# Scores of units 8 to 15 in two column halves, with q times its exponents made on POOL

## The chip, the cores and the metric

The kernel runs on one core of one Trainium2 chip. A core has TensorE (PE, matmuls; its weight loads are listed as PEld), VectorE (DVE), ScalarE (ACT), GpSimd (POOL) and SyncE (SP, which here issues DMAs alone). Each engine works through its own list of instructions in order; semaphores tie the lists together. The metric is the device time of one execution in microseconds (us). All times in the traces count from the first instruction of the profiled execution.

## The reference

A gated linear attention (mLSTM) over batch 4, 8 heads, 768 positions and head size 40, and behind it two dense two-layer networks, 320 to 2048 to 320 features, on all 3072 rows:

```python
for t in range(S):
    m_new = np.maximum(f_gate[:, :, t] + m, i_gate[:, :, t])
    f_stab = np.exp(f_gate[:, :, t] + m - m_new)
    i_stab = np.exp(i_gate[:, :, t] - m_new)
    C = f_stab[:, :, None, None] * C + i_stab[:, :, None, None] * np.einsum('bhd,bhe->bhde', vt, kt)
    n = f_stab[:, :, None] * n + i_stab[:, :, None] * kt
    h_tilde = np.einsum('bhde,bhe->bhd', C, qt)
    nq = np.einsum('bhd,bhd->bh', n, qt)[:, :, None]
    y[:, :, t] = o * h_tilde / np.maximum(np.abs(nq), 1.0)
...
h = x @ w_in;  g = h * np.clip(h + 3.0, 0.0, 6.0) / 6.0;  x = g @ w_out      # first network
h = x @ w_in;  r = np.maximum(h, 0.0);  g = r * r;        x = g @ w_out      # second network
```

## The kernel before

**Attention in units.** The 768 positions are cut into 12 chunks of 64. A unit is one chunk of one batch element, all 8 heads: 48 units, numbered so that each batch element's chunks come in order. For unit u the steps are, by their names in the code: at_qk (SP loads q and k, transposed, into the tile qkt, three buffers), at_kn and at_va (loads of k and v), w_pe and w_e up to unit 15 (PE sums gates into PSUM, ACT takes the exponent into the tile W, four buffers) or at_gload, w_add, w_mask and w_e from unit 16 on (SP, POOL, POOL, ACT), at_S (PE: the scores), at_P and x_q (fill the tile Xm, two buffers), x_k (fills its right part with k times the last exponents), at_Y (PE: Xm against the tile Z of v and carried state), at_C (copies the new state), at_n1 to at_n3 (divide, and multiply with the output gate). The first 64 rows of Xm hold the masked, weighted scores, the next 40 rows hold q times its exponents.

**Three ways to the same Xm.** Up to unit 15 (U1), at_S makes, for each head, a score product into rows 0 to 63 of the PSUM tile Sp (L448) and a product of q with an identity into rows 64 to 103 (L450), and at_P multiplies all 104 rows with W in one DVE instruction (L472). Units 16 to 21 have only the score products (L463), the even heads in rows 0 to 63 of Sp and the odd heads in rows 64 to 127, so that Sp is half as wide; at_P has two halves (L479), and x_q multiplies q and W straight out of SBUF (L412), on POOL unless FIRST says otherwise. From unit 22 (US) on the scores are made from split operands (L456).

**The two networks.** A slot s is one group of 128 hidden features for a group of rows. mm_A makes its hidden values in PSUM (ring ps_a, two tiles), act1 (ACT), act1b (DVE), act2 (ACT or DVE) and act2b (DVE) form the activation as a high and a low part, mm_B multiplies these with the second weights two slots later. act2b gives the PSUM tile of mm_A back for slots up to 23. Weights come as 64 bit numbers: w_load (SP), w_exp (ACT), w_b1 and w_b2 (DVE), w_hi (ACT or DVE), w_lo (POOL or DVE); they are all loaded while the first attention units run. The other gates' steps (gate_b:1 is L310 and L311 on DVE) and at_rg (POOL, L348) run in the same stretch.

**The order.** No scheduler chooses it. The string FIRST lists steps for the first part of the program by hand, and what is not in it follows by the rule in moe(). Each engine executes its instructions in the order in which this list names them; @v, @g and @a send a step to DVE, POOL or ACT. A tile of a ring (qkt, W, Xm, Sp) is given to a new unit when the last instruction that uses the old one is over, and the instruction that writes it first waits for that. Waits between engines are put in from the data alone.

Around the change FIRST reads, in part: "at_qk:12 act2:9@v", "at_rg:12 ... gate_b:1 ... act2:11 x_k:9@v at_kn:12 at_S:10 act1:12 w_b2:0,12 o_load:5 at_Y:9 act2b:11 x_k:10 w_hi:0,12", and later "at_S:12 ... at_qk:15 ... at_va:19 ... w_load:0,15 ... x_k:12@v w_exp:0,15 x_k:13@v at_gload:16 ... act1:18 at_Y:12 w_b1:0,15 ... act1b:18".

Of the kernel before, what the change touches and what calls it, by code (L numbers as in the profile page):

```python
# [38 lines left out]
at_Y:1 at_rg:4 w_load:0,3 at_C:0@v at_n1:0 w_load:0,10 at_n2:0@a w_load:0,9 w_pe:4 at_rg:5@v  # L39
at_kn:4 at_n1:1 at_n3:0@g at_S:2 at_n2:1 at_C:1@v x_k:2 at_va:6 w_hi:0,0 at_n3:1@g w_exp:0,1 w_pe:5  # L40
at_P:2,0 w_e:4 at_rg:6 at_S:3 w_load:0,4 at_qk:5 w_lo:0,0@v w_exp:0,7 w_b1:0,1 at_Y:2 w_e:5
w_b2:0,1 w_exp:0,2 at_qk:6 at_P:3,0 x_k:3 w_pe:6 w_hi:0,1 at_n1:2 at_rg:7 at_n2:2@a at_S:4
w_load:0,8 w_b1:0,2 w_b2:0,2 at_C:2 w_pe:7 w_exp:0,3 at_rg:8@v at_kn:5 at_P:4,0 at_n3:2@g w_hi:0,2
at_Y:3 w_e:7 w_lo:0,2 w_e:6 t_pe:0,0,0 at_n1:3 at_kn:6 w_exp:0,9 at_C:3@v w_load:0,6 t_hi:0,0,0
at_n2:3@a at_va:7 at_n3:3 t_lo:0,0,0 x_k:4 t_pe:0,0,1 w_lo:0,1 w_exp:0,10 at_Y:4 t_hi:0,0,1@v
at_va:8 t_lo:0,0,1 w_exp:0,4 at_va:9 w_b1:0,3 at_qk:7 mm_A:0 at_C:4 w_b1:0,4 at_n1:4 w_b2:0,4
mm_A:1 act1:0 at_kn:7 at_n2:4 w_hi:0,4 at_va:10 act1b:0 at_S:5 at_n3:4@g act2:0@v at_qk:8 act1:1
act2b:0 w_exp:0,8 w_lo:0,4 act1b:1 mm_A:2 at_P:5,0 act2:1 mm_B:0,1 act2b:1 act1:2 w_load:0,11
at_S:6 w_exp:0,6 w_b2:0,3 at_qk:9 mm_A:3 x_k:5@v w_hi:0,3 act1b:2 x_k:6 at_kn:8 at_Y:5 at_P:6,0
act2:2 w_load:0,5 w_lo:0,3 act1:3 mm_B:0,0 at_va:11 act2b:2 at_C:5 at_S:7 act1b:3 at_va:12 at_n1:5  # L50
act2:3 at_n2:5 x_k:7 at_qk:10 mm_A:4 at_P:7,0 at_kn:9 at_Y:6 w_exp:0,11 w_b1:0,6 load_gates:1
w_b2:0,6 w_pe:8 act1:4 mm_B:1,0 at_C:6 mm_B:2,0 act2b:3 at_rg:9 w_e:8 mm_B:1,1 act1b:4 w_hi:0,6
mm_B:2,1 at_n1:6 w_pe:9 at_rg:10 at_n2:6 act2:4 mm_B:3,1 w_exp:0,5 act2b:4 mm_B:3,0 at_n3:6 w_e:9
mm_A:5 w_b1:0,5 w_lo:0,6@v at_Y:7 act1:5 o_load:3 w_b2:0,5 at_S:8 x_k:8@a at_qk:11 at_n1:7 mm_A:6
at_P:8,0 o_load:2 at_C:7 act1b:5 w_pe:10 at_rg:11 w_hi:0,5 w_load:0,13 w_b1:0,8 o_load:1 at_n3:5
# [9 lines left out]
o_load:5 at_Y:9 act2b:11 x_k:10 w_hi:0,12 at_kn:13 at_P:10,0 mm_A:13 at_C:9 w_lo:0,12 act1b:12
at_va:17 mm_B:11,3 at_n1:9 act2:12 mm_B:11,2 at_n2:9 at_qk:13 act1:13 at_S:11 act1b:13 at_n3:9@g
act2b:12 act2:13 at_Y:10 act2b:13 at_va:18 w_b2:0,9 mm_A:14 at_C:10 gate_bT:1 w_hi:0,9 at_qk:14
mm_A:15 act1:14 x_k:11@v o_load:4 mm_B:12,2 act1b:14 w_lo:0,9 act1:15 at_kn:14 mm_B:12,3 at_P:11,0
act2:14 mm_B:13,3 mm_B:13,2 act2b:14 w_pe:12 w_b1:0,10 mm_A:16 act1b:15 at_rg:13 w_e:12 at_n1:10
act2:15 at_n2:10@a act2b:15 w_b1:0,14 at_S:12 w_b2:0,14 act1:16 mm_A:17 at_qk:15 w_b2:0,10  # L70
w_hi:0,14 act1b:16 w_lo:0,14 mm_B:14,2 at_P:12,0 act1:17 mm_B:15,2 act2:16@v mm_B:14,3 w_pe:13
act1b:17 at_rg:14 mm_B:15,3 w_e:13 act2b:16 at_Y:11 act2:17 w_hi:0,10@v w_pe:14 at_va:19 at_C:11@v
at_rg:15 mm_B:16,3 w_e:14 mm_B:16,1 at_n1:11 mm_B:16,2 at_n2:11@a w_lo:0,10 act2b:17 w_load:0,15
at_S:13 mm_B:17,3 at_P:13,0 at_qk:16 mm_B:16,0 mm_B:17,0 w_b1:0,11 w_pe:15 w_b2:0,11 mm_A:18 w_e:15
at_n3:11 w_hi:0,11 x_k:12@v w_exp:0,15 x_k:13@v at_gload:16 mm_B:17,2 at_n3:10 at_kn:15 act1:18
at_Y:12 w_b1:0,15 at_va:20 mm_A:19 act1b:18 w_lo:0,11 at_C:12 at_n1:12 at_kn:16 at_n2:12@a
at_gload:17 act2:18@v w_add:16 at_S:14 act2b:18 w_b2:0,15 mm_B:18,3 act1:19 at_qk:17 at_Y:13
w_b1:0,13 w_hi:0,15 mm_A:20 w_b2:0,13 at_va:21 at_C:13 x_k:14@a at_n1:13 w_add:17 at_n2:13 act1b:19
mm_B:17,1 w_mask:16 mm_B:18,1 at_P:14,0 act2:19 mm_B:18,0 at_kn:17 w_mask:17 mm_B:18,2 at_gload:18
w_e:16 act2b:19 at_S:15 act1:20 at_n3:12 at_n3:13 w_hi:0,13 mm_B:19,3 at_qk:18 mm_B:19,0 at_P:15,0  # L80
x_k:15@a w_lo:0,13 mm_B:19,2 act1b:20 at_S:16 at_Y:14 w_lo:0,15@v act2:20 mm_A:21 at_kn:18 at_va:22
at_n1:14 w_add:18 w_e:17 act2b:20 at_gload:19 at_C:14 at_n2:14 w_mask:18 mm_A:22 act1:21 x_q:16
# [13 lines left out]
act1b:27 act1:28 at_S:20 at_n3:19@g at_qk:23 act1b:28 mm_B:24,0 mm_B:25,0 x_k:20 at_P:20,0  # L96
mm_B:25,3 at_P:20,1 mm_B:26,0 qk_split:22 at_S:21 mm_B:26,3 mm_A:29 x_q:21@v x_k:21@a mm_B:25,1
mm_B:24,2 at_P:21,0 mm_B:25,2 act2:27@v mm_B:26,2 mm_B:26,1 act2b:27 mm_A:30 at_P:21,1 act1:29
at_kn:22 act2:28@v at_va:26 act2b:28 at_gload:23 mm_B:27,2 act1b:29 mm_B:27,3 qk_split:23 at_qk:24
mm_B:28,2 mm_A:31 act2:29 act1:30 at_S:22 act1b:30 w_add:23 at_Y:20 mm_A:32 act2b:29 at_C:20  # L100
at_n1:20 w_mask:23 act1:31 at_n2:20@a x_q:22 at_P:22,0 mm_B:29,2 act1b:31 mm_B:27,0 at_S:23
at_n3:20@g mm_B:28,0 w_e:23 at_kn:23 mm_B:29,0 x_k:22@a at_kn:24 mm_B:27,1 at_gload:24 mm_B:28,3
act2:30@v at_Y:21 at_gload:25 act2b:30 at_gload:26 mm_B:29,3 qk_split:24 mm_B:28,1 at_qk:25
mm_B:30,2 act1:32 mm_B:30,3 mm_B:29,1 act2:31 mm_B:30,0 mm_B:30,1 mm_A:33 act1b:32 w_add:24
at_n1:21 at_n2:21 w_mask:24 act2:32@v mm_A:34 w_add:25 w_e:24 at_C:21@v act2b:31 at_Y:22 act2b:32
act1:33 mm_B:31,3 at_C:22@v x_q:24 act1:34 mm_B:32,3 act1b:33 at_va:27 mm_B:31,1 mm_B:32,1 at_kn:25
act1b:34 act2:33 w_mask:25 mm_A:35 at_n1:22 w_add:26 qk_split:25 w_e:25 mm_A:36 at_n2:22 x_q:23
x_k:23@a mm_B:31,0 mm_B:32,0 at_P:23,0 at_qk:26 mm_B:31,2 t_pe:0,2,0 act2b:33 act2:34 at_Y:23
x_k:24@v t_hi:0,2,0 mm_B:33,1 act2b:34 act1:35 mm_B:33,3 mm_B:33,0 t_lo:0,2,0 at_n3:22@g at_C:23
mm_B:34,3 act1:36 act1b:35 mm_B:34,0 w_mask:26 mm_B:34,1 act1b:36 t_pe:0,2,2 mm_B:32,2 w_e:26  # L110
at_n3:21 mm_B:33,2 at_n1:23 t_hi:0,2,2 mm_B:34,2 at_n2:23 act2:35 mm_A:37 t_lo:0,2,2 at_n3:23@g
act2:36 act2b:35 t_pe:0,2,3 mm_A:38 at_qk:27 act2b:36 t_hi:0,2,3 act1:37 t_lo:0,2,3 act1b:37
t_pe:0,2,1 act1:38 mm_B:35,2 mm_A:39 t_hi:0,2,1 act1b:38 act2:37 t_lo:0,2,1 act2b:37 mm_A:40
act1:39 act1b:39 at_S:24 mm_B:35,3 at_P:24,0 qk_split:26 mm_B:35,0 at_gload:27 mm_B:35,1 at_kn:26
at_Y:24 act2:38 at_kn:27 mm_B:36,1 at_S:25 mm_B:36,2 at_n1:24 x_q:26 mm_B:37,2 at_C:24@v mm_B:37,1
at_n2:24 mm_B:36,3 act2b:38 mm_B:37,3 mm_B:36,0 at_n3:24 mm_B:37,0 act2:39@v x_q:25 x_k:25@a
x_k:26@a at_P:25,0 act2b:39
# [749 lines left out]
```

## Time and profile before

| | us |
|---|---|
| median of 3 timed runs | 842.63 (841.74 to 842.73) |
| span of the profiled execution | 839.9 |
| PE busy in it | 812.8 (97%) |
| DVE busy | 548.6 (65%) |
| ACT busy | 428.2 (51%) |
| POOL busy | 222.6 (27%) |

The span runs from the first to the last instruction of the program. A share of busy time is an average over stages: the attention units lie in the first 400 us, and the weights of the first network are prepared in the first 125 us. To read the profile for one stage, take the windows of that stage, and then the list of each engine.

### The profile page before, as it was taken

How to read it: one execution, taken by the hardware profiler on the slowest of the kernel's cores; microseconds unless marked ns; L12 is line 12 of the kernel's file. 1: busy time of each engine (PE TensorE's matmuls, PEld its weight loads, DVE VectorE, ACT ScalarE, POOL GpSimd, SP SyncE). 2: the span in 40 equal slices, each digit the busy share in tenths (PEclk: the TensorE clock that was granted, in tenths of full speed). 3: DMA queues.
4: the chain of work that ended last, by engine and by line, in shares of the span. 5: the costliest groups of instructions: out<-in, count | busy, mean ns of one | idle time of the engine just before them, and what ended most of it. 6: DMA issues, size and time to landing. Idle time of an engine off the chain costs nothing.

```text
span 839.9 us, 19200 instructions
## 1 busy us (share of the span) xinstructions
PE 812.8 (97%) x7968; PEld 719.5 (86%) x7968; DVE 548.6 (65%) x919; ACT 428.2 (51%) x815; POOL 222.6 (27%) x201
## 2 busy tenths in 40 slices
...
GB/s 240 280 150 210 108 115 80 132 87 26 123 95 117 84 112 100 87 119 7 2 81 181 197 94 1 1 33 1 32 0 1 32 1 1 32 1 1 32 1 31
DMA packets 28674, 63.59 MB, mean 76 GB/s; under 512 B 4748, under 2 KB 17100, under 8 KB 28588
## 3 DMA queue, kind: packets, MB, share of 16 engines
...
q14 instruction: 24, 0.20, 0.1%
...
## 4 chain that ended last, share of the span: by engine, by line
PE 92%; ACT 2%; DVE 2%; issue 2%; POOL 1%; DMA 0%; ACTq 0%; POOLq 0%; DVEq 0%
PE hps L639 41%; PE acc L680 39%; PE Yp L490 4%; PE tp L615 2%; PE Sp L456 2%; PE Sp L448 1%; PE Wp L372 1%; PE Sp L450 1%; PE Wp L370 1%; PE Sp L463 0%; ACT qs L432 0%; ACT X L687 0%; ACT yt L519 0%; DMA qkt<-in_qk 0%; POOL Xm L412 0%
## 5 line engine op out<-in xcount | busy, mean ns | idle before, releaser
L639 PE MATMUL hps<-xs,wi 128*128 128x512 f32 (+1 forms) x1600 | 389.4, 386 | 1.5 <-DVE xs L624 0.7
L680 PE MATMUL acc<-wo,gh 128*128 128x320 f32 x1536 | 348.2, 313 | 0.0
L639 PEld LDWEIGHTS hps<-xs,wi 128*128 128x128 f32 x1600 | 287.3, 190 | 51.1 <-DVE xs L624 1.1
L680 PEld LDWEIGHTS acc<-wo,gh 128*128 128x128 f32 x1536 | 259.1, 188 | 9.8
L680 PE MATMUL acc<-wo,gl 128*128 128x320 f32 x768 | 237.5, 309 | 0.5 <-DVE gl L670 0.5
L670 DVE TENSOR_TENSOR gl<-g,gh 128x512 fp32r<-128x512 f32 x176 | 131.1, 746 | 65.9 <-ACT gh L665 64.7
L660 DVE TENSOR_TENSOR g<-g 128x512 f32<-128x512 f32 x96 | 66.4, 691 | 127.8 <-ACT g L650 127.2
L680 PEld LDWEIGHTS acc<-wo,gl 128*128 128x128 f32 x768 | 144.4, 188 | 0.7 <-DVE gl L670 0.7
L665 ACT CAST gh<-g 128x512 fp32r<-128x512 f32 x169 | 104.6, 619 | 66.4 <-DVE g L660 53.3
L648 ACT ACTIVATE g<-hps,three 128x512 f32<-128x512 f32 (+1 forms) x104 | 68.0, 654 | 137.3 <-PE hps L639 122.0
L650 ACT ACTIVATE g<-hps 128x512 f32<-128x512 f32 x96 | 57.4, 598 | 151.6 <-PE hps L639 151.6
L657 DVE SCALAR_TENSOR_TENSOR g<-g,hps 128x512 f32<-128x512 f32 x80 | 54.7, 685 | 50.2 <-ACT g L648 50.0
L412 POOL TENSOR_TENSOR Xm<-qkt,W 40x512 f32<-40x512 f32 x31 | 40.9, 1321 | 109.2 <-ACT W L402 83.5
L600 POOL TENSOR_TENSOR wi<-wt,wi 128x768 fp32r<-128x768 f32 x14 | 26.6, 1897 | 106.9 <-ACT wi L595 101.7
L379 POOL TENSOR_TENSOR W<-W,bT 104x512 f32<-104x512 f32 x32 | 43.2, 1348 | 17.3 <-DMA W<-Gd 13.1
L490 PEld LDWEIGHTS Yp<-Z,Xm 104*32 104x32 f32 (+1 forms) x3072 | 35.0, 110 | 14.0 <-issue 11.5
L434 DVE SCALAR_TENSOR_TENSOR qs<-qs,less,qkt 120x512 fp32r<-120x512 f32 x52 | 38.0, 772 | 8.5 <-ACT qs L432 8.3
L490 PE MATMUL Yp<-Z,Xm 104*32 104x41 f32 (+1 forms) x3072 | 40.9, 209 | 1.0 <-issue 0.9
L615 PE MATMUL tp<-ident,X 128*128 128x128 f32 x144 | 24.4, 279 | 8.9 <-DVE xs L626 6.0
L600 POOL TENSOR_TENSOR wo<-wt,wo 128x640 fp32r<-128x640 f32 x15 | 24.4, 1630 | 31.5 <-ACT wo L595 31.4
L615 PEld LDWEIGHTS tp<-ident,X 128*128 128x128 f32 x144 | 18.7, 143 | 14.7 <-ACT rwi L574 6.4
L532 DVE TENSOR_TENSOR X<-X,yt 64x320 f32<-64x320 f32 x34 | 28.7, 845 | 2.5 <-ACT yt L519 1.6
...
## 6 DMA issues: line engine op xcount, KB each, us to landing
...
```

What stands on the lines that cost most here:

```text
L379: on("w_add", "g", u).tensor_tensor(out=W, in0=W, in1=bT[:, c - NC1, b * H:(b + 1) * H].unsqueeze(2).to_broadcast([KX, H, L]), op=ALU.add)
L490: nc.tensor.matmul(out=Yp[o:e, h, :], lhsT=Xm[:, h, o:e], rhs=Z[b][c % 2][:, h, :], start=True, stop=True)
L600: on("w_lo", "g", ph, i).tensor_tensor(out=w[:, 1], in0=f, in1=w[:, 0].bitcast(F32), op=ALU.subtract)
L615: nc.tensor.transpose(out=tp[:, k, :], in_=x[:, c0:c0 + P], identity=ident)
L639: nc.tensor.matmul(out=h, lhsT=w[:, hl, kk, o:o + P], rhs=t[:, xk, i0 * P:i1 * P], start=(i == 0), stop=(i == len(TERMS) - 1))
L648: nc.scalar.activation(out=g, in_=T["h", s], func=ACTF.Relu, bias=three)
L650: nc.scalar.activation(out=g, in_=T["h", s], func=ACTF.Relu)
L657: nc.vector.scalar_tensor_tensor(out=g, in0=r, scalar=6.0, in1=T["h", s], op0=ALU.min, op1=ALU.mult)
L660: nc.vector.tensor_tensor(out=g, in0=r, in1=r, op=ALU.mult)
L665: copy("act2", s)(out=gh, in_=g)
L670: nc.vector.tensor_tensor(out=gl, in0=g, in1=gh.bitcast(F32), op=ALU.subtract)
L680: nc.tensor.matmul(out=acc[i], lhsT=g[:, n], rhs=w[:, hl, m % MG, :], start=(m == 0 and q == 0), stop=(m == NM - 1 and q == 2))
```

## The change

Units 8 to 15 take the second way instead of the first: at_S without the identity products and with a half as wide Sp, at_P in two halves, and x_q as an instruction of its own on POOL. In the code the limit in at_S, at_P and x_q is the new U2 = 8 in place of U1 = 16; w_e and the other uses of U1 stay. In FIRST, x_q:u is put right in front of x_k:u, and at_P:u,1 right behind at_P:u,0, for u from 8 to 15; nothing else in the list is moved (the rest of that part of the diff is lines broken at other places).

```diff
+at_Y:1 at_rg:4 w_load:0,3 at_C:0@v at_n1:0 w_load:0,10 at_n2:0@a w_load:0,9 w_pe:4 at_rg:5@v at_kn:4
...
+w_lo:0,6@v at_Y:7 act1:5 o_load:3 w_b2:0,5 at_S:8 x_q:8 x_k:8@a at_qk:11 at_n1:7 mm_A:6 at_P:8,0
+at_P:8,1 o_load:2 at_C:7 act1b:5 w_pe:10 at_rg:11 w_hi:0,5 w_load:0,13 w_b1:0,8 o_load:1 at_n3:5
...
+w_e:11 mm_A:12 gate_b:1 mm_B:10,2 mm_B:10,3 act2:11 x_q:9 x_k:9@v at_kn:12 at_S:10 act1:12 w_b2:0,12
+o_load:5 at_Y:9 act2b:11 x_q:10 x_k:10 w_hi:0,12 at_kn:13 at_P:10,0 at_P:10,1 mm_A:13 at_C:9
...
+w_hi:0,9 at_qk:14 mm_A:15 act1:14 x_q:11 x_k:11@v o_load:4 mm_B:12,2 act1b:14 w_lo:0,9 act1:15
...
+mm_B:16,2 at_n2:11@a w_lo:0,10 act2b:17 w_load:0,15 at_S:13 mm_B:17,3 at_P:13,0 at_P:13,1 at_qk:16
+mm_B:16,0 mm_B:17,0 w_b1:0,11 w_pe:15 w_b2:0,11 mm_A:18 w_e:15 at_n3:11 w_hi:0,11 x_q:12 x_k:12@v
+w_exp:0,15 x_q:13 x_k:13@v at_gload:16 mm_B:17,2 at_n3:10 at_kn:15 act1:18 at_Y:12 w_b1:0,15
...
+w_add:16 at_S:14 act2b:18 w_b2:0,15 mm_B:18,3 act1:19 at_qk:17 at_Y:13 w_b1:0,13 w_hi:0,15 mm_A:20
+w_b2:0,13 at_va:21 at_C:13 x_q:14 x_k:14@a at_n1:13 w_add:17 at_n2:13 act1b:19 mm_B:17,1 w_mask:16
...
+at_P:15,1 x_q:15 x_k:15@a w_lo:0,13 mm_B:19,2 act1b:20 at_S:16 at_Y:14 w_lo:0,15@v act2:20 mm_A:21
...
@@ -174,6 +175,7 @@
     UL = 4
 
     US = 22
+    U2 = 8
     KS = 3 * D
...
     def x_q(u):
-        if u < U1:
+        if u < U2:
             return
...
         pool, tag = (ps_a, "a") if u in (1, 2) else (ps_s, "s")
-        if u < U1:
+        if u < U2:
 
             Sp = pool.tile([P, H, L], F32, tag=tag, name="Sp")
...
         W, Xm, Sp = T["W", u], x_tile(u), T["S", u]
-        if u < U1:
+        if u < U2:
             if o == 0:
```

## Rows read from the trace of the kernel before

**Rows 1.** Page, part 4: the chain that ended last, shares by engine.

```profile
PE 92%; ACT 2%; DVE 2%; issue 2%; POOL 1%; DMA 0%; ACTq 0%; POOLq 0%; DVEq 0%
```

**Rows 2.** Windows: stretch, length, busy PE, PEld, DVE, ACT, POOL; clock, DMA, GB/s.

```profile
77.00:92.00 15.00, 15.00 (x296) 13.65 (x295) 14.05 (x29) 10.64 (x19) 7.52 (x5) 1.00 0.34 90
...
104.00:115.00 11.00, 11.00 (x160) 8.82 (x161) 10.09 (x19) 5.85 (x18) 4.99 (x4) 1.00 0.40 127
...
72.80:76.00 3.20, 3.20 (x14) 3.20 (x15) 3.14 (x6) 3.15 (x10) 1.35 (x3) 0.52 0.92 231
```

**Rows 3.** Timeline of PE: start, length, engine, line, operation, tiles, shape, count.

```profile
85.42 0.27 PE L448 MATMUL Sp<-qkt 40*64 40x64 f32 x1
...
86.50 0.80 PE L490 MATMUL Yp<-Z,Xm 104*32 104x41 f32 x64
87.23 1.22 PE L639 MATMUL hps<-xs,wi 128*128 128x256 f32 x8
...
115.41 0.56 PE L680 MATMUL acc<-wo,gh 128*128 128x320 f32 x2
115.81 0.31 PE L680 MATMUL acc<-wo,gl 128*128 128x320 f32 x1
```

**Rows 4.** Chain of waits, in order of time: start, length, what; at_S of a later unit.

```profile
143.98 0.61 PE Sp L463 x16
```

**Rows 5.** Timeline of PE near 72 us; in brackets the idle time and its releaser.

```profile
70.44 0.55 PE L615 MATMUL tp<-ident,X 128*128 128x128 f32 x3 [2.88 <-POOL X L532]
```

**Rows 6.** Lines L472, L479, L412 by source: ns min/median/max, first and last start, shapes.

```profile
L472 DVE TENSOR_TENSOR Xm<-Sp,W x16: 673/690/693, 13.6 to 121.8; 104x512 f32<-104x512 f32 x16
...
L479 DVE TENSOR_TENSOR Xm<-Sp,W x12: 407/422/426, 126.3 to 163.6; 64x256 f32<-64x256 f32 x12
...
L412 POOL TENSOR_TENSOR Xm<-qkt,W x31: 1287/1294/1735, 126.0 to 391.9; 40x512 f32<-40x512 f32 x31
```

**Rows 7.** Timelines of POOL and DVE near 105 us.

```profile
104.60 1.84 POOL L600 TENSOR_TENSOR wi<-wt,wi 128x768 fp32r<-128x768 f32 x1
...
104.77 1.70 DVE L506 TENSOR_SCALAR rd<-rd 64x8 int32<-64x8 int32 x1
```

**Rows 8.** Timeline of DVE, 81 to 91 us.

```profile
81.56 1.26 DVE L580 TENSOR_SCALAR wt<-rwo 128x640 int32<-128x640 int32 x1
...
83.39 0.67 DVE L310 TENSOR_TENSOR X<-X,X 32x512 f32<-32x512 f32 x1
84.10 0.68 DVE L311 TENSOR_TENSOR X<-X,X 32x512 f32<-32x512 f32 x1
84.71 0.47 DVE L423 TENSOR_TENSOR Xm<-kI,W 104x320 f32<-104x320 f32 x1
...
85.98 0.41 DVE L670 TENSOR_TENSOR gl<-hps,gh 128x256 fp32r<-128x256 f32 x1
...
90.50 0.83 DVE L586 SCALAR_TENSOR_TENSOR wt<-rwo,wt 128x640 int32<-128x640 int32 x1
```

**Rows 9.** Timeline of POOL, 80 to 91 us.

```profile
80.36 2.11 POOL L348 TENSOR_TENSOR pre<-pre,Gp 64x512 fp32r<-64x512 f32 x1
82.54 0.87 POOL L423 TENSOR_TENSOR Xm<-kI,W 104x320 f32<-104x320 f32 x1
...
89.46 0.85 POOL L532 TENSOR_TENSOR X<-X,yt 64x320 f32<-64x320 f32 x1 [0.62 <-DVE yt L522]
```

**Rows 10.** Waits of SyncE's queue, whole span: us in total, times, longest.

```profile
SPq L332 <- POOL Xm L412: 6.5, 3, 3.3
```

**Rows 11.** Timeline of SyncE's DMA issues: at_qk:15 and w_load:0,15.

```profile
98.70 0.28 SPq L332 DMA_DIRECT2D qkt<-in_qk  x1
...
104.58 0.54 SPq L562 DMA_DIRECT2D rwo<-in_w1o  x1
```

**Rows 12.** Timeline of ACT: w_exp:0,15.

```profile
110.52 0.78 ACT L574 ACTIVATE rwo<-rwo 128x640 f32<-128x640 f32 x1
```

**Rows 13.** Timeline of DVE: act2b:18.

```profile
114.83 0.69 DVE L670 TENSOR_TENSOR gl<-hps,gh 128x512 fp32r<-128x512 f32 x1
```

More of the change, by code (lines that the diff above doesn't have):

```diff
@@ L38 @@
 w_exp:0,0 at_P:1,0 w_pe:3 x_k:1 w_e:2 at_Y:0 w_b1:0,0 w_e:3 w_b2:0,0 at_kn:3 o_sig:0 w_load:0,2
[L39 to L55, printed above, removed]
+at_Y:1 at_rg:4 w_load:0,3 at_C:0@v at_n1:0 w_load:0,10 at_n2:0@a w_load:0,9 w_pe:4 at_rg:5@v at_kn:4
@@ new lines @@
+w_exp:0,4 at_va:9 w_b1:0,3 at_qk:7 mm_A:0 at_C:4 w_b1:0,4 at_n1:4 w_b2:0,4 mm_A:1 act1:0 at_kn:7
+at_n2:4 w_hi:0,4 at_va:10 act1b:0 at_S:5 at_n3:4@g act2:0@v at_qk:8 act1:1 act2b:0 w_exp:0,8
+w_lo:0,4 act1b:1 mm_A:2 at_P:5,0 act2:1 mm_B:0,1 act2b:1 act1:2 w_load:0,11 at_S:6 w_exp:0,6
+w_b2:0,3 at_qk:9 mm_A:3 x_k:5@v w_hi:0,3 act1b:2 x_k:6 at_kn:8 at_Y:5 at_P:6,0 act2:2 w_load:0,5
+w_lo:0,3 act1:3 mm_B:0,0 at_va:11 act2b:2 at_C:5 at_S:7 act1b:3 at_va:12 at_n1:5 act2:3 at_n2:5
+x_k:7 at_qk:10 mm_A:4 at_P:7,0 at_kn:9 at_Y:6 w_exp:0,11 w_b1:0,6 load_gates:1 w_b2:0,6 w_pe:8
@@ L65 @@
[L65 to L82, printed above, removed]
```

74 lines of the change are left out of this document (46 added, 28 removed).

## The prediction

> **What bounds the kernel now.** I read the chain of work that ended last first: 92% of it is TensorE [rows 1], so a microsecond taken from TensorE is a microsecond of the run, wherever TensorE has no gap. Then the windows over the stretch in which units 9 to 15 run (77 to 125 us): in 77 to 92 and in 104 to 115 us TensorE is busy for 15.00 of 15.00 and 11.00 of 11.00 us, at the full clock (2.4 GHz). VectorE (DVE) stands beside it with 14.05 and 10.09 us [rows 2]. So TensorE is the bound by a hair only: in the first window DVE has 0.95 us left in 15. What the change puts on DVE, or between DVE and its inputs, is as important as what it takes from TensorE. Last I read the queues one by one, in the order of FIRST, to see where the new POOL instruction falls and who stands behind it.
>
> **What is removed: the identity products.** Unit 10's 32 matmul records (16 scores, 16 identity products) begin at 85.42 and the next step, at_Y:9, begins at 86.50: 1.08 us [rows 3]. A unit that makes scores alone (from 16 on) takes 0.61 us on the chain [rows 4]. The saving is 0.47 us a unit. Unit 8 gives nothing: TensorE stands still a little later in any case, 2.88 us before 70.44 for x_T's input [rows 5], and that wait comes down a chain through ScalarE. Units 9 to 15 could give 7 x 0.47 = 3.3 us.
>
> A rule of the Trainium skill speaks against this saving. "TensorEngine Tiling (Array Packing)", Tiling Modes, says that different tiles of the array work in parallel; score and identity product go to different output columns, so by it the identity products cost nothing and the saving is 0 instead of 3.3 us. The trace sides with a saving: 1.08 against 0.61 us.
>
> **What is added on DVE.** at_P was one instruction of 690 ns and becomes two of 422 ns [rows 6]. The halves overlap a little; I take +0.17 us a unit (0 to 0.3), about 1.2 us for seven units. They read PSUM and one SBUF tile and wait for no POOL work in the rows.
>
> **What is added on POOL.** x_q is 1.29 us a unit [rows 6], in the queue right before x_k's place. POOL has idle time for it. The price is elsewhere. A DVE instruction that reads two SBUF tiles, or a tensor_scalar on SBUF, doesn't run while a POOL instruction that reads SBUF does: a 64x8 tensor_scalar issued at 104.77 ended 1.70 us later, with the POOL instruction of 104.60 [rows 7]. Both sides wait: POOL's 2.11 us instruction at 80.36 lies around one DVE tensor_scalar and holds up the next, which ends at 82.82 [rows 8, 9]. They take turns, one instruction each.
>
> **Units 9 and 10.** x_q:9, x_q:10 and x_k:10 now stand in POOL's queue one behind another, after at_rg:12, which ends at 82.47. Their inputs are long there. On DVE gate_b:1 (L310, L311) and x_k:9 (L423) come at the same time, all on two SBUF tiles. Taking turns from 82.82: x_q:9 to 84.11, L310 (0.67) to 84.78, x_q:10 to 86.07, L311 (0.68) to 86.75, x_k:10 (0.87) to 87.62, x_k:9 (0.47) to 88.09 instead of 85.18 [rows 8, 9]. DVE is then 2.9 us late. at_Y:9 needs x_k:9 and can't begin before 88.1, where it began at 86.50; and mm_A:13, at 87.23 before, needs the PSUM tile that act2b:11 (L670 at 85.98, ended 86.39) gives back, now at 89.3 [rows 3, 8]. So TensorE stands 2.1 us **behind** the old run at mm_A:13, with the saving of units 9 and 10 gone into the wait. Bounds: if DVE got both its L310 and L311 in between without a turn for POOL, 0.7 us on DVE alone and no loss on TensorE; with every turn against it, 2.9 us less the 0.84 us of slack in front of mm_A:13, so 0 to +2.1. I take 2.1, because the rows show turns.
>
> **Unit 11.** x_q:11 follows at_n3:9 (89.46, 0.85 us) directly; w_b2's L586, two SBUF tiles, was issued 0.19 us behind that [rows 8, 9] and now waits up to 1.1 us for x_q:11. TensorE saves 0.47 us at unit 11 and is pushed by DVE again. I leave it at +2.1 us near 95 (bounds +1.0 to +3.3).
>
> **The load queue.** The tile qkt has three buffers, and at_qk:u+3 takes that of unit u. Before, its last reader was at_S:u; now it is also x_q:u. SyncE issues in order, so it stands still until x_q:u is over: it already does so for later units, 6.5 us in three waits [rows 10]. In the list x_q stands behind the at_qk that takes its buffer for units 9 and 11 to 15. For most of them nothing else is late. For unit 12 it is: at_qk:15 went out at 98.70, after at_S:12 [rows 11]. x_q:12 stands on POOL behind w_lo:0,10, which ends at 106.44 [rows 7], so it ends at 107.8 at the earliest, and at_qk:15 is 9.1 us late. Queued behind it are at_va:19, which nobody needs soon, and w_load:0,15, at 104.58 before [rows 11] and now at about 108.7. ScalarE used that load at 110.52 [rows 12], so it lands at most 5.9 us after the start of its issue; its 0.66 MB at the 127 GB/s of that window [rows 2] are 5.2 us. I take 4.5 us (3 to 5.9): it lands at 113.2. ScalarE works in order as well: act1:18 stands right behind w_exp:0,15, and on DVE w_b1:0,15, which needs it, stands in front of act1b:18. After w_exp (0.78, to 114.0) DVE has w_b1, act1b, the short at_n1:12, act2 and act2b, the long ones some 0.7 us each (act2b 0.69), 3 us in all: act2b:18 ends at about 117.0, not at 115.52 [rows 12, 13], and mm_B:18, which began at 115.41 and took act2b's result from 115.81 [rows 3], is 1.2 us late (0 to 2.7: by the old distance of 5.0 us from w_exp's start to act2b's end it would be 118.2). All that is reckoned as if POOL were on its old time. It isn't: the chain to w_lo:0,10 runs through DVE and ScalarE, which by then are between 1.2 and 3.3 us late. With 2.3 us in the middle TensorE is 1.2 + 2.3 = **3.5 us late** at mm_B:18. That contains the earlier 2.1 us; they are not added, since the same lateness runs through both.
>
> **After that.** Unit 15 saves 0.47 us, the four at_P halves of units 14 and 15 and turns against x_q:14 and x_q:15 cost as much. From 125 us on nothing is changed, and TensorE has no gap in which 3.5 us could be made up. The other waits that x_q adds, at_Y:u on POOL and the W buffers of at_gload:16 to 19, end before the x_k or at_P of the same unit does, so they cost nothing while x_k is late; without that cover the worst is one x_q, 1.29 us.
>
> **Sum.** The profiled span is 839.9 us and the median of the timed runs 842.6, 2.7 us around it, which I keep. 839.9 + 3.5 = 843.4 us of span, 842.6 + 3.5 = 846.1 us timed.
>
> **Rivals.**
> (a) *Only TensorE counts.* DVE and POOL find their turns in idle time and the load lands in time: 842.6 - 3.3 = 839.3. For it: TensorE is the chain. Against it: 0.95 us of idle DVE in 77 to 92 us. Chance 0.12.
> (b) *Only one of the two delays is real*, either the turns at units 9 and 10 or the load that comes late. Then one delay of 1 to 2 us stands against two to four savings of 0.47: about +0.5, 843.1 us. This is also the case in which SyncE isn't held by x_q. Chance 0.22.
> (c) *The clock falls.* TensorE would stand 2.5 us before at_Y:9 and some 3 us before mm_B:18. Before, after standing 2.88 us up to 70.44, it was granted 0.52 of its clock, the lower level of 1.2 GHz, from 72.8 to 76 us [rows 2, 5]; the 13 matmuls of that stretch would have taken some 1.7 of its 3.2 us at the full clock, so each time costs about 1.5 us. With two, 846.1 + 3.0 = 849.1. It decides only where the waits do come. Chance 0.20.
> (d) *The identity products were free.* Then nothing is given back at units 12, 13 and 15, 3 x 0.47 = 1.4 us: 847.5. The rows speak against it (1.08 against 0.61 us). Chance 0.03. This is the result that the rule on array tiles would give.
>
> **How the numbers follow.** Forecast 0.43, (a) 0.12, (b) 0.22, (c) 0.20, (d) 0.03. The likeliest is 846.1. The range runs from 841.0 (part of the savings with a small delay) to 851.0 (the clock falls and the upper bounds of the delays). About 0.2% (1.7 us) is what a measurement of this kernel can tell from no change: faster is (a), 0.12; the same is nearly all of (b), 0.21; slower is the rest, 0.67.
>
> **What would show it.** In the changed kernel: at_S of units 9 to 15 at 0.61 us; x_q and L310, L311, L423 taking turns near 83 to 88 us, at_Y:9 beginning near 88 us and a gap in TensorE before it; at_qk:15 behind x_q:12; w_load:0,15 near 110; a wait of ScalarE in front of w_exp:0,15; a gap before mm_B:18. Wrong would be: no gap in TensorE between 77 and 125 us (then (a)), w_load:0,15 still near 104 (then the queue step), or L310 and L311 at 0.67 us beside running POOL work (then the turns).

## The result and the profile after

The changed kernel took 853.04 us (median of 4 runs, 852.11 to 853.42) beside 842.44 us for the kernel before on the same chip: a ratio of 1.012, 95% interval 1.0108 to 1.0132. It is **10.6 us slower**. The forecast was 846.1 us with a range of 841 to 851: the sign was right, the size was not. The profiled span is 851.6 us, 11.7 us over the one before: the profile of the changed kernel is of the longest of its four runs and the one before of the shortest of its three, so the two spans lie further apart than the medians. One of the four runs of units_9_15 below (1319.6 us) was disturbed and is left out of its time and ratio.

Line numbers of the changed kernel are two higher (x_q is L414, x_k L425, at_P in halves L481, at_Y L492, act2b L672); in most kernels of the experiments they are three higher. "Late" below means: start of an instruction in the profiled execution less its start in the kernel before.

The chain that ended last, by engine (page of after, part 4), beside [rows 1]: DVE has 8% of it where it had 2%, DMA 3% where it had 0%.

```profile
PE 83%; DVE 8%; issue 3%; DMA 3%; ACT 2%; POOL 1%; SPq 1%; DVEq 0%; ACTq 0%; POOLq 0%
```

Windows of after, columns as in [rows 2]:

```profile
77.00:92.00 15.00, 12.58 (x175) 10.84 (x175) 14.57 (x25) 10.85 (x19) 10.03 (x7) 1.00 0.19 48
104.00:115.00 11.00, 10.15 (x128) 7.74 (x126) 10.48 (x18) 4.97 (x14) 10.69 (x7) 1.00 0.12 30
115.00:125.00 10.00, 8.22 (x158) 6.27 (x159) 7.63 (x13) 5.70 (x17) 3.63 (x3) 0.83 0.58 145
125.00:147.00 22.00, 20.14 (x254) 17.27 (x253) 18.21 (x37) 12.38 (x36) 15.59 (x16) 0.84 0.29 76
```

TensorE was without a gap in the first two windows; now it has gaps, while DVE is busy for 14.57 of 15.00 us. In the last two windows the granted clock is below full as well: 0.83 and 0.84, where the kernel before had 1.00 in both.

TensorE's own timeline shows where it falls behind: mm_A:13, at_Y:12 (broken off and taken up again), mm_A:19, mm_B:18, at_S:15.

```profile
89.60 1.10 PE L641 MATMUL hps<-xs,wi 128*128 128x256 f32 x7 [0.41 <-DVE gl L672]
...
114.27 0.27 PE L492 MATMUL Yp<-Z,Xm 104*32 104x41 f32 x4
116.24 0.84 PE L492 MATMUL Yp<-Z,Xm 104*32 104x41 f32 x60 [1.70 <-DVE Xm L425]
117.01 3.59 PE L641 MATMUL hps<-xs,wi 128*128 128x512 f32 x8
121.65 0.53 PE L682 MATMUL acc<-wo,gh 128*128 128x320 f32 x2 [0.43 <-DVE gh L667]
...
129.09 0.68 PE L465 MATMUL Sp<-qkt 40*64 40x64 f32 x16 [1.86 <-issue]
...
134.05 5.44 PE L641 MATMUL hps<-xs,wi 128*128 128x512 f32 x16
139.33 0.49 PE L617 MATMUL tp<-ident,X 128*128 128x128 f32 x3
```

Against [rows 3] TensorE is 2.4 us late at mm_A:13 (89.60 for 87.23) and 6.2 us at mm_B:18 (121.65 for 115.41); 4.9 us more come behind that, where the prediction had nothing. By 142 us it is 11.1 us late, and that stays to the end.

The load queue, as SyncE issued it, and ScalarE behind it, beside [rows 11, 12]:

```profile
112.29 0.28 SPq L334 DMA_DIRECT2D qkt<-in_qk  x1
...
113.19 0.58 SPq L564 DMA_DIRECT2D rwo<-in_w1o  x1
```

```profile
118.31 0.79 ACT L576 ACTIVATE rwo<-rwo 128x640 f32<-128x640 f32 x1 [4.61 <-DMA rwo<-in_w1o]
```

at_qk:15 goes out 13.6 us late and w_load:0,15 8.6 us; ScalarE stands 4.61 us for it. SyncE's waits for x_q, beside [rows 10], went from 6.5 us in 3 waits to:

```profile
SPq L334 <- POOL Xm L414: 26.8, 8, 10.9
```

### The profile page after: what moved, and what is told of

The parts are those of the page before. It is cut to its first block, busy times and chain, and to the rows that moved or that the text cites. A ratio compares the mean times of both kernels' runs of the same rounds, so it can differ in the third digit from the quotient of the medians.

```text
span 851.6 us, 18973 instructions
## 1 busy us (share of the span) xinstructions
PE 815.7 (96%) x7840; PEld 719.9 (85%) x7840; DVE 561.2 (66%) x927; ACT 427.9 (50%) x815; POOL 235.4 (28%) x209
## 4 chain that ended last, share of the span: by engine, by line
PE 83%; DVE 8%; issue 3%; DMA 3%; ACT 2%; POOL 1%; SPq 1%; DVEq 0%; ACTq 0%; POOLq 0%
PE hps L641 38%; PE acc L682 36%; PE Yp L492 3%; PE tp L617 2%; PE Sp L458 2%; DMA rwo<-in_w1o 1%; DVE gl L672 1%; DVE qs L436 1%; PE Wp L374 1%; DVE wt L582 1%; DVE X L534 1%; ACT qs L434 0%; PE Sp L465 0%; DMA kI<-in_kn 0%; PE Wp L372 0%
## 5 line engine op out<-in xcount | busy, mean ns | idle before, releaser
L672 DVE TENSOR_TENSOR gl<-g,gh 128x512 fp32r<-128x512 f32 x176 | 131.1, 746 | 66.4 <-ACT gh L667 64.7
L414 POOL TENSOR_TENSOR Xm<-qkt,W 40x512 f32<-40x512 f32 x39 | 52.3, 1343 | 110.1 <-ACT W L404 79.1
L492 PEld LDWEIGHTS Yp<-Z,Xm 104*32 104x32 f32 (+1 forms) x3072 | 35.8, 111 | 16.3 <-issue 12.1
L492 PE MATMUL Yp<-Z,Xm 104*32 104x41 f32 (+1 forms) x3072 | 42.0, 211 | 3.1 <-DVE Xm L425 1.7
L534 DVE TENSOR_TENSOR X<-X,yt 64x320 f32<-64x320 f32 x34 | 32.3, 954 | 2.5 <-ACT yt L521 1.6
L425 POOL TENSOR_TENSOR Xm<-kI,W 104x320 f32<-104x320 f32 x32 | 28.4, 889 | 5.4 <-DVE pre L350 3.0
```

The costliest lines, as they stand in the source:

```text
L414: on("x_q", "g", u).tensor_tensor(out=x_tile(u)[E0:KX, :, 0:L], in0=T["qk", u][E0:KX, 0], in1=T["W", u][E0:KX], op=ALU.mult)
L492: nc.tensor.matmul(out=Yp[o:e, h, :], lhsT=Xm[:, h, o:e], rhs=Z[b][c % 2][:, h, :], start=True, stop=True)
L672: nc.vector.tensor_tensor(out=gl, in0=g, in1=gh.bitcast(F32), op=ALU.subtract)
```

## Experiments

The theory going in had three parts: turns between POOL's x_q and DVE in units 9 to 13, the load w_load:0,15 held back behind x_q:12, and a clock that falls where TensorE has stood. The rival was that the halves (scores and at_P) themselves cost time. The kernels fall into four questions; the times are medians, each with its ratio to the kernel before on the same chip (842.0 to 842.4 us).

### Which units, and is it the load?

**load_first.** One token of FIRST moved:

```diff
-act1:16 mm_A:17 at_qk:15 ... act2b:17 w_load:0,15 at_S:13
+act1:16 mm_A:17 w_load:0,15 at_qk:15 ... act2b:17 at_S:13
```

> The change, with one token moved: w_load:0,15 is issued on SP in front of at_qk:15 and so no longer stands behind SP's wait for x_q:12. Theory of the load queue (the second and larger delay is the weights of w_load:0,15 landing late, 118.2 us in the changed kernel): mm_B:18 starts about 3.5 us earlier than in the changed kernel, TensorE is then some 2.5 to 4 us behind the kernel before at that place instead of 6.2, and of the 10.6 us of the whole change 3.5 to 7 go, the larger figure if the clock that fell behind it stays up: 846 to 849.5 us. Theory that turns between POOL and DVE are the whole of it: nothing changes by this move, 853 us. Theory that the scores in halves themselves cost TensorE or DVE time: 853 us as well.

849.23 us, ratio 1.0076 (1.0061 to 1.009): 3.8 us of the 10.6 go, within the 3.5 to 7 of the theory of the load queue. mm_B:18 starts at 119.19, 3.8 us late instead of 6.2. So the load is a cause, but 6.9 us stay. Two waits are left as they were: at_Y:12's 1.70 us and at_S:15's, now 2.04.

```profile
115.81 0.79 PE L492 MATMUL Yp<-Z,Xm 104*32 104x41 f32 x60 [1.70 <-DVE Xm L425]
116.52 2.12 PE L641 MATMUL hps<-xs,wi 128*128 128x512 f32 x8
...
119.19 0.56 PE L682 MATMUL acc<-wo,gh 128*128 128x320 f32 x2
...
126.53 0.68 PE L465 MATMUL Sp<-qkt 40*64 40x64 f32 x16 [2.04 <-issue]
...
134.16 0.49 PE L617 MATMUL tp<-ident,X 128*128 128x128 f32 x3
```

mm_A:19 takes 2.12 us here and 3.59 in the changed kernel: that is the clock. Windows of after, then of this kernel:

```profile
118.00:122.00 4.00, 3.57 (x25) 2.51 (x23) 2.67 (x7) 2.77 (x9) 0.00 (x0) 0.72 0.82 157
130.00:138.00 8.00, 8.00 (x100) 6.66 (x99) 5.20 (x12) 3.98 (x13) 5.51 (x5) 0.57 0.43 112
```

```profile
118.00:122.00 4.00, 4.00 (x92) 3.05 (x91) 3.95 (x5) 3.32 (x11) 2.81 (x2) 1.00 0.43 119
130.00:138.00 8.00, 8.00 (x153) 6.84 (x138) 7.48 (x17) 4.12 (x8) 6.91 (x7) 1.00 0.35 106
```

Much of the stretch from 118 to 122 us and nearly all of 130 to 138 us is at the lower level (1.2 GHz) in the changed kernel, and none of it is here. That is one execution of load_first, of 847.84 us with a mean clock of 0.996. Its three others took 849.21 to 849.35 us with mean clocks of 0.982 to 0.994; no trace of them shows where their clock fell.

**units_8_11** and **units_12_15**: the condition names the units. (For units_12_15 `NEW = (12, 13, 14, 15)`.)

```diff
+    NEW = (8, 9, 10, 11)
-        if u < U2:
+        if u < U1 and u not in NEW:
```

> The change for units 8 to 11 alone; units 12 to 15 keep the identity products and x_q is not made for them. Theory of two separate delays: the first one is all here (TensorE 2.4 us behind at mm_A:13, 3.1 at w_pe:12), the second one is not, w_load:0,15 is issued near 104.6 us as before plus those 2 to 3 us; the end is 2 to 4 us behind the kernel before, 844.5 to 846.5 us. Theory that halves cost nothing and only the load queue delays: 841 to 842.5 us. Theory that every unit adds its share (10.6 us over eight units): about 5.3 us, 847.7 us.

845.09 us, 1.0031 (1.0021 to 1.004): 2.8 us, as two separate delays would have it. TensorE is 2.5 us late at mm_A:13.

> The change for units 12 to 15 alone; units 8 to 11 keep the identity products. Theory of two separate delays: TensorE is where it was in the kernel before until about 106 us (shift within 0.5 us), then at_qk:15 waits for x_q:12 on SP, w_load:0,15 is issued at 108 to 111 us instead of 104.6, x_k:12 takes turns with POOL, and mm_B:18 is 3 to 5 us late; the end is 5 to 8 us late, 847.5 to 850.5 us. Theory that the second delay only passes on the lateness of units 9 to 11: within 1.5 us of the kernel before. Theory that every unit adds its share: about 847.7 us, but with a shift that grows evenly from unit 12 on.

846.84 us, 1.005 (1.0035 to 1.0065): 4.5 us, below what was expected (5 to 8) in the time. The step itself is there, with no lateness from units 8 to 11: TensorE is on the old time at mm_A:19 (112.28 us) and stands 3.46 us before mm_B:18.

```profile
110.65 0.59 SPq L565 DMA_DIRECT2D rwo<-in_w1o  x1
```

```profile
115.16 0.76 ACT L577 ACTIVATE rwo<-rwo 128x640 f32<-128x640 f32 x1 [3.69 <-DMA rwo<-in_w1o]
```

```profile
118.46 0.81 PE L683 MATMUL acc<-wo,gh 128*128 128x320 f32 x2 [3.46 <-DVE gh L668]
```

**u12_15_load_first**: units 12 to 15 with the move of load_first.

> The change for units 12 to 15 alone, with w_load:0,15 issued in front of at_qk:15. Without that move (units 12 to 15 alone) w_load:0,15 went out at 110.65, w_exp:0,15 waited 3.69 us for it and mm_B:18 3.46 us, and TensorE was 4.1 us behind the kernel before at mm_B:18's successor. Theory of the load queue: this wait goes, TensorE is at most 2 us behind at 117 us, the end is 843 to 845.5 us. Theory that the wait is made by turns between x_q:12, x_q:13 and DVE: 846 to 847 us, as without the move.

845.07 us, 1.0036 (1.0024 to 1.0048). ScalarE no longer waits for the load, and the wait before mm_B:18 falls from 3.46 to 1.82 us. The time moves by 1.8 us, and the two intervals just overlap. The clock has a part in that: behind the 3.46 us the profile of units_12_15 has 0.57 of it granted from 118 to 122 us, and this one 1.00. What is left, 2.7 us, is not the load.

### What does unit 8 do?

In the changed kernel TensorE is 1.4 us late at 79 us already, before x_q:9 has started. One DVE instruction stands out, at_n3:5 at L532 (after: L534). DVE before and after, and below each POOL:

```profile
63.09 0.48 DVE L532 TENSOR_TENSOR X<-X,yt 64x320 f32<-64x320 f32 x1
```

```profile
63.48 1.55 POOL L600 TENSOR_TENSOR wo<-wt,wo 128x640 fp32r<-128x640 f32 x1 [6.33 <-ACT wo L595]
```

```profile
63.42 1.85 DVE L534 TENSOR_TENSOR X<-X,yt 64x320 f32<-64x320 f32 x1
```

```profile
63.40 1.54 POOL L602 TENSOR_TENSOR wo<-wt,wo 128x640 fp32r<-128x640 f32 x1 [4.56 <-ACT wo L597]
```

Before, DVE was 0.39 us ahead of POOL's w_lo:0,5 and took 0.48 us. After, DVE comes 0.33 us later, POOL is 0.02 us ahead, and DVE waits it out: 1.85 us. A small push turns the order round and costs 1.4 us.

**units_9_15** (`NEW = (9, ..., 15)`) and **unit_8** (`NEW = (8,)`):

> The change for units 9 to 15; unit 8 stays the old way. In the changed kernel X<-X,yt of at_n3:5 on DVE comes 0.33 us later than before (63.42 instead of 63.09 us, behind x_q:8 and the second at_P:8), now stands behind the POOL product w_lo:0,5 that starts at 63.40, and takes 1.86 us instead of 0.48; TensorE is 1.4 us late at 79 us already. Theory that this first lateness is unit 8's: without it at_n3:5 takes 0.48 us again, TensorE is within 0.8 us of the kernel before at 79 us, and the end is 1 to 2 us before the changed kernel's, 851 to 852 us. Theory that the lateness at mm_A:13 is made by units 9 and 10 alone: 853 us, and 2.4 us late at mm_A:13 as before.

849.71 us (three runs, 847.29 to 850.43; the profile is of the shortest), 1.008 (1.0065 to 1.0096): 3.3 us less than the whole change, more than expected. at_n3:5 takes 0.48 us again. And mm_A:13 is 0.57 us late, not 2.4 (0.06 us in u9_15_load_first below, which is the same program up to there), although the turns of units 9 and 10 are there, on POOL and DVE:

```profile
81.45 3.00 POOL L415 TENSOR_TENSOR Xm<-qkt,W 40x512 f32<-40x512 f32 x2
```

```profile
83.88 1.11 DVE L313 TENSOR_TENSOR X<-X,X 32x512 f32<-32x512 f32 x1
85.02 1.11 DVE L314 TENSOR_TENSOR X<-X,X 32x512 f32<-32x512 f32 x1
86.07 0.47 DVE L426 TENSOR_TENSOR Xm<-kI,W 104x320 f32<-104x320 f32 x1
```

```profile
87.80 1.21 PE L642 MATMUL hps<-xs,wi 128*128 128x256 f32 x8 [0.33 <-DVE gl L673]
```

> The change for unit 8 alone. Theory that unit 8 makes the first lateness, since x_q:8 and the second at_P:8 push DVE's at_n3:5 (X<-X,yt) by 0.33 us behind the start of POOL's w_lo:0,5: at_n3:5 takes 1.8 us instead of 0.48, TensorE is 1.2 to 1.8 us behind the kernel before at 79 us and 1 to 2 us at mm_A:13, and the end is 0.8 to 2 us late, 843.1 to 844.3 us. Theory of the prediction, that unit 8 gives and takes nothing as TensorE stands still up to 70 us in any case: 842.3 us, and less than 0.8 us behind at 79 us.

843.39 us, 1.0013 (1.0004 to 1.0021): unit 8 alone costs 1.1 us, by the same order of DVE and POOL (at_n3:5 took 1.85 us at 63.48, w_lo:0,5 began at 63.45). The lateness at 79 us itself is not a safe measure: in the kernel with units 14 and 15 alone, where nothing is changed up to there, one profiled execution is 1.4 us late at 79 us too, with 0.57 of the clock granted in 70 to 73 us, where the kernel before had 0.91. The times and the row of at_n3:5 carry this point.

### Do turns follow the place of x_q?

**early**: unit 8 the old way, each x_q further ahead on POOL.

```diff
+at_rg:11 x_q:9 ... w_lo:0,7 x_q:10 ... x_q:11 at_n3:9@g ... w_e:12 x_q:12
+w_lo:0,10 x_q:13 ... w_add:16 x_q:14 ... at_C:13 x_q:15
```

> The change for units 9 to 15 (unit 8 is left the old way), with each x_q moved to an earlier place on POOL, right behind the exponents it reads: x_q:9 behind at_rg:11, x_q:10 behind w_lo:0,7, x_q:11 ahead of at_n3:9, x_q:12 behind w_e:12, x_q:13 behind w_lo:0,10, x_q:14 behind w_add:16, x_q:15 behind at_C:13. Theory that the delays come from where x_q stands on POOL (its turns with DVE's work ahead of x_k, and SP held behind x_q:12) and that the halves themselves are a gain of 0.3 us a unit: 840 to 842.5 us, no slower than the kernel before, w_load:0,15 issued by 106 us. Theory that the halves cost time whatever the place of x_q, or that x_q takes its turns wherever it stands: 845 to 850 us.

845.16 us, 1.0032 (1.0021 to 1.0044): 4.6 us better than units 9 to 15 at their places (849.71), but not as good as expected. x_q:9, now at 60.81, made DVE's at_n3:5 late in the way that x_q:8 does, so the gain of leaving unit 8 out was lost.

**early2**: the same, with x_q:9 behind w_lo:0,5 instead of in front of it.

> As the kernel with each x_q early (units 9 to 15, unit 8 the old way), but x_q:9 stands behind w_lo:0,5 instead of in front of it, so that at_n3:5 on DVE comes before POOL's w_lo:0,5 again. Theory that a small delay of DVE in front of at_n3 lets POOL's w_lo go first and costs 1.3 us each time: at_n3:5 takes 0.48 us at 63 us, at_n3:10 or 11 takes 0.48 us near 111 us as x_q:13 is not beside L586 there any more, and the end is 839.5 to 842 us. Theory that the order at at_n3:5 does not reach the end: 845 us as with the other early places.

844.17 us, 1.0018 (1.0009 to 1.0028): at_n3:5 is back at 0.48 us, and mm_A:14 is 0.08 us late. The end is not where it was expected. x_q:13 still meets DVE near 110 us. DVE and POOL:

```profile
108.60 1.79 DVE L589 SCALAR_TENSOR_TENSOR wt<-rwo,wt 128x640 int32<-128x640 int32 x1
...
111.52 1.84 DVE L535 TENSOR_TENSOR X<-X,yt 64x320 f32<-64x320 f32 x1
```

```profile
108.30 1.41 POOL L415 TENSOR_TENSOR Xm<-qkt,W 40x512 f32<-40x512 f32 x1
111.29 1.71 POOL L603 TENSOR_TENSOR wo<-wt,wo 128x640 fp32r<-128x640 f32 x1 [1.59 <-ACT wo L598]
```

L589 waits for x_q:13, the 1 us that it loses puts the next at_n3 0.23 us behind w_lo:0,11, and that costs another 1.35 us: the same turn-round as at 63 us.

**u9_15_load_first**: units 9 to 15 at their places, with the load moved.

> The change for units 9 to 15, with w_load:0,15 issued in front of at_qk:15: neither unit 8's lateness nor the late load. Units 9 to 15 alone took some 850 us, and the move alone took 3.8 us from the whole change. Theory that the two causes are separate and add: 845.5 to 847 us, with TensorE within 0.8 us of the kernel before at mm_A:13 and a wait of 1 to 2 us left near 112 to 117 us for turns of x_q:12 and x_q:13 with DVE. Theory that one lateness runs through both, so that without unit 8 the load is not late enough to matter: 848 to 850 us, as without the move.

847.48 us, 1.0064 (1.005 to 1.0077): between the two expectations, 2.2 us below units 9 to 15 without the move, with intervals that overlap. Read together: without unit 8 and with the load in time 5.5 us are left, and the early places (early2) take 3.7 of these away. What they take away are turns and the fall of the clock behind them, which no run here parts: in u9_15_load_first TensorE stands 1.68 us in the middle of at_Y:12, and the granted clock is 0.68 in 114 to 118 us and 0.50 in 118 to 122; in early2 at_Y:12 isn't broken off, and the clock is 1.00 in both.

**units_14_15** (`NEW = (14, 15)`):

> The change for units 14 and 15 alone. In the changed kernel at_S:15 waits 1.86 us for its PSUM tile, which at_P:14 gives back late, behind w_b1, w_b2 and at_n1 on DVE beside w_add:16, x_q:14 and w_add:17 on POOL. Theory that x_q:14 alone brings this about by its turns: a wait of 1 to 2 us before at_S:15 and 1 to 2.5 us at the end, 843.3 to 844.8 us. Theory that the wait only comes where DVE and POOL are already late from units 8 to 13, so that they work at the same things side by side: no wait over 0.5 us there, 842 to 843 us.

842.50 us, 0.9998 (0.9988 to 1.0007): no loss. The wait of at_S:15 (1.86 us in the changed kernel, 2.04 with the load moved) is 0.53 us here. It comes from earlier lateness that brings x_q:14 beside other DVE work, not from units 14 and 15 by themselves.

### What are the halves worth?

**xq_memset**: on POOL a memset of the same rows stands in x_q's place for units 8 to 15.

```diff
+        if u < U1:
+            nc.gpsimd.memset(x_tile(u)[E0:KX, :, 0:L], 1.0)
+            return
```

> The change, but on POOL the place of x_q:8 to x_q:15 is taken by a memset of the same rows of the exponent tile with ones: q times the exponents of these units is left out, so POOL reads no SBUF there and qkt has no reader behind at_S. The scores in halves without identity products and the two at_P of each unit stay as in the change. Theory that POOL's x_q makes the whole loss, by turns with DVE and by holding SP: what is left is the gain of TensorE less the second half of at_P, 3.3 less 1.2 us at the most, 839.3 to 841.5 us. Theory that the halves on DVE and TensorE cost time of their own: 843 to 850 us.

842.30 us, 1.0001 (0.9992 to 1.0011). With x_q's product gone the whole 10.6 us are gone, so POOL's x_q is what costs, by its turns and by the queue that it holds. But no gain is left either. The row that explains part of it: the memset is no free stand-in. DVE, then POOL:

```profile
80.78 2.07 DVE L585 TENSOR_SCALAR wt<-rwi 128x768 int32<-128x768 int32 x1
```

```profile
80.20 1.29 POOL L350 TENSOR_TENSOR pre<-pre,Gp 64x512 fp32r<-64x512 f32 x1
81.43 1.00 POOL L415 MEMSET Xm<- 40x512 f32 x2
```

**oneP_memset**: as xq_memset, but the scores of all eight heads in one tile, and one at_P.

```diff
+        elif u < U1:
+            Sp = pool.tile([P, H, L], F32, tag=tag, name="Sp")
+            for h in range(H):
+                nc.tensor.matmul(out=Sp[0:L, h, :], lhsT=qkt[E0:KX, 1, h, :], rhs=qkt[E0:KX, 0, h, :], ...)
...
-        if u >= US:
+        if u < U1 or u >= US:
```

> As the kernel with the memset in place of x_q (q times the exponents of units 8 to 15 is left out), but the scores of units 8 to 15 stay in one tile of all eight heads, and at_P is one DVE instruction of 64x512 again, some 690 ns, instead of two of 422 ns. TensorE still makes 16 products a unit instead of 32. Theory that the second half of at_P on DVE (0.17 us a unit, 1.4 us in all) ate the gain of TensorE: 840.5 to 841.3 us. Theory that in these stretches DVE paces, so that what TensorE saves turns into its waits for DVE whatever at_P looks like: 841.8 to 842.6 us, no different from the kernel before.

844.63 us, 1.0028 (1.0018 to 1.0039). **Neither theory held**: 2.3 us slower than with halves. TensorE's timeline says why. Scores of one unit and the step behind them, here and in xq_memset:

```profile
86.08 1.14 PE L460 MATMUL Sp<-qkt 40*64 40x64 f32 x16
87.16 0.80 PE L501 MATMUL Yp<-Z,Xm 104*32 104x41 f32 x64
```

```profile
86.27 0.68 PE L468 MATMUL Sp<-qkt 40*64 40x64 f32 x16
86.88 0.80 PE L495 MATMUL Yp<-Z,Xm 104*32 104x41 f32 x64
```

16 scores without identity products, all in the same output columns, take 1.08 us from the first to the next step, exactly what 16 scores with 16 identity products took [rows 3]. In two column halves the same 16 take 0.61. So **the identity products were free**, and the 0.47 us comes from the halves. It also shows that the halves do bring something: 2.3 us (with the two intervals, 1.1 to 3.5) of the 8 x 0.47 = 3.8 that TensorE saves. By subtraction the memsets then cost 2.4 us against the kernel before, since in oneP_memset TensorE and at_P (some 690 ns) take what they took there; no run shows that price by itself.

**oneP_early2**: early2 with one tile and one at_P.

> The change for units 9 to 15 with the early places of x_q (x_q:9 behind w_lo:0,5, x_q:12 behind w_e:12, x_q:13 behind w_lo:0,10 and so on), and one at_P of 64x512 a unit instead of two halves; unit 8 the old way. With halves this took 844.2 us. Theory that turns of x_q:13 with DVE near 110 us and the later ones make the loss: 843.5 to 844.5 us. Theory that the second halves of at_P make it: 842.3 to 843.2 us.

846.17 us, 1.0044 (1.0025 to 1.0063): again above both expectations, and 2.0 us above early2. But its eight runs spread with the clock: the three with a mean clock of 0.996 took 843.59 to 843.79 us, no more than early2's with that clock (843.43 to 844.45), and the five with 0.977 to 0.993 took 846.16 to 849.46. So this pair doesn't price the halves; xq_memset and oneP_memset, which differ by 2.3 us at like clocks too, do.

**memset_early**: halves for units 9 to 15, with the memsets where POOL is idle.

> Scores in halves and two at_P for units 9 to 15, unit 8 the old way; q times the exponents of these units is left out, and in its place POOL fills the rows with ones by a memset of some 0.52 us, put where POOL is idle (behind w_lo:0,5, w_lo:0,7, at_rg:13, w_lo:0,10, w_lo:0,11 and so on), so that DVE's tensor_scalar near 80.8 us no longer waits for two of them. TensorE makes seven units in 0.61 us instead of 1.07, 3.2 us less. Theory that TensorE is the bound once POOL is out of the way: 839.5 to 841 us. Theory that DVE, with 1.2 us more for the second halves, paces this stretch and TensorE's gain turns into its waits for DVE: 841.6 to 843 us.

841.95 us, 0.9999 (0.999 to 1.0008), within the range of the theory that DVE paces. TensorE's 0.46 us can be read at three units (its lateness falls from 1.46 to 0.08 us between 84 and 98 us), but nothing reaches the end: 1.3 us were lost between 64 and 79 us (where the kernel with units 14 and 15 alone, unchanged up to there, lost 0.8) and 0.5 us near 120 us. The first loss is where the clock differs: 0.50 granted in 76 to 79.5 us, where the kernel before had 1.00. Among the runs with a mean clock of 0.995 or 0.996, seven of each kernel, the medians are 841.8 and 842.4 us, so a small gain may be there; it isn't shown. In 77 to 125 us TensorE was busy for 48.00 of 48.00 us before, DVE for 43.52; in this kernel:

```profile
77.00:125.00 48.00, 46.76 (x718) 39.41 (x716) 45.26 (x88) 33.35 (x85) 26.19 (x23) 0.97 0.35 101
```

### The losses in order

| Kernel | against before, us | what was taken away |
|---|---|---|
| the change | +10.6 | |
| units_9_15 | +7.3 | unit 8 |
| u9_15_load_first | +5.5 | the late load |
| early2 | +1.8 | places of x_q among DVE's work (and the late load) |
| memset_early | 0.0 | x_q's reading on POOL |

The steps are differences of medians and depend on their order: unit 8 alone is 1.1 us, the load taken from the whole change 3.8, and each holds what the clock lost or kept with it. No version was found that is faster than the kernel before.

## Why the prediction was right and wrong

**Which engine bounds.** "By a hair only" was right: TensorE's gain of 3.8 us for eight units came through to 2.3 us at best, and DVE's lateness came through wherever TensorE had no slack in front of it.

**The identity products: right size, wrong cause.** I compared 1.08 us for a unit with identity products with 0.61 us for a later unit without [rows 3, 4], and put the difference down to the products. The two differ in a second thing, the column halves, and oneP_memset shows that this is the whole of it. "TensorEngine Tiling (Array Packing)", Tiling Modes, of the Trainium skill says that different tiles work in parallel. I wrote that the trace speaks against it; it agrees: 1.08 us with and without the products. Rival (d) had the right mechanism, and was priced as if nothing else gave a gain. The sum wasn't hurt, since the halves are part of the change.

**at_P** was right: two halves take 0.84 us (units 9 to 15, after), one took 0.69.

**Unit 8 gives nothing: wrong.** I looked at TensorE's wait before 70.44 us [rows 5] and concluded that lateness there is absorbed. It isn't for DVE: x_q:8 and the second half of at_P:8 push at_n3:5 behind w_lo:0,5. Alone that is 1.1 us, in the whole change 3.3.

**Units 9 and 10: right number, wrong account.** Forecast were x_k:9 done at 88.09 and mm_A:13 2.1 us late. Measured were 88.34 and 2.4:

```profile
85.70 1.09 DVE L312 TENSOR_TENSOR X<-X,X 32x512 f32<-32x512 f32 x1
86.82 1.12 DVE L313 TENSOR_TENSOR X<-X,X 32x512 f32<-32x512 f32 x1
87.87 0.47 DVE L425 TENSOR_TENSOR Xm<-kI,W 104x320 f32<-104x320 f32 x1
```

The turns are in the rows. But TensorE was 1.4 us late at 82 us already, before x_q:9 began at 83.28. And with unit 8 the old way (units_9_15) x_k:9 ends at 86.54, which is 1.4 us late, not 2.9, and mm_A:13 is 0.57 us late, as TensorE was at 82 us: the 0.84 us of slack took what the turns added. So most of the 2.4 us came through unit 8, which I had at nothing, and two errors cancelled: the number was right by luck. The overcharge: I had x_q:9 and x_q:10 take their turns from 82.82 to 86.07; in units_9_15 they began at 81.45 and were over at 84.45.

**Unit 11** stayed within its bounds: 3.2 us late at w_pe:12.

**The load queue: right mechanism, size off.** SyncE did stand behind x_q:12 (10.9 us, the longest of the eight waits). The mis-sized term is POOL's lateness by then. The prediction took 2.3 us; w_lo:0,10 began at 108.81 instead of 104.60 [rows 7], 4.2 us late:

```profile
108.81 1.84 POOL L602 TENSOR_TENSOR wi<-wt,wi 128x768 fp32r<-128x768 f32 x1
110.73 3.38 POOL L414 TENSOR_TENSOR Xm<-qkt,W 40x512 f32<-40x512 f32 x2
114.18 1.66 POOL L602 TENSOR_TENSOR wo<-wt,wo 128x640 fp32r<-128x640 f32 x1
```

From its issue at 113.19 to ScalarE's start at 118.31 the load took 5.1 us, within 3 to 5.9. mm_B:18 came 6.2 us late instead of 3.5; load_first puts up to 2.4 us of that on the load, where the prediction had 1.2.

**A term that was left out.** DVE's x_k:12 fell beside w_lo:0,11 (114.18 above). Its row holds x_k:12 and x_k:13 and takes 2.21 us for two instructions of 0.47:

```profile
114.38 2.21 DVE L425 TENSOR_TENSOR Xm<-kI,W 104x320 f32<-104x320 f32 x2
```

TensorE stood 1.70 us in the middle of at_Y:12 for it. I had counted turns of x_q with DVE, but not turns of DVE with POOL instructions that were there already and now fall elsewhere.

**"After that": the step that failed most.** I had nothing lost from mm_B:18 on; it was 4.9 us. First, at_S:15 had to wait 1.86 us for its PSUM tile, which at_P:14 gave back late: at_P:14 ends at 128.99 and at_S:15 begins at 129.09.

```profile
128.13 0.86 DVE L481 TENSOR_TENSOR Xm<-Sp,W 64x256 f32<-64x256 f32 x2
```

Then the clock fell, which was rival (c) at 0.20. From at_S:15 to the transposes at 139.33 the changed kernel took 10.2 us, where load_first, at the full clock, took 7.6 (126.53 to 134.16); mm_A:21 and 22 alone took 5.44 us for 3.92. So this one fall cost 2.6 us, where the rival had 1.5. The fall before it, in mm_A:19 (3.59 us for 2.12), cost little by itself: mm_B:18 behind it waited for gh in any case, at the end of the chain from the late w_exp:0,15. A rival that needs only the waits that the forecast itself has should have been put into the forecast: with this fall alone at its measured price that would have been 848.7 us. The rest of the miss lies in the waits: 2.7 us more up to mm_B:18 than forecast, and at_S:15's.

**The sum.** The 2.7 us between the span and the median before are not time around the span: the 839.9 us belong to the run of 841.74 us, and 1.8 us lie around it. The forecast in timed us doesn't depend on it.
